# Moving the conversion of the first weights from the end of an attention phase to all of it

## The chip, the cores and the metric

One core of one Trainium2 chip runs the whole program. The metric is the device time of one execution in microseconds (us). The kernel before takes 809.04 us, the median of three runs (808.77 to 810.95).

## The reference, cut to what matters

Three layers follow each other, all in 32-bit floating point. The first is an attention in which a query sees only the keys that fall into the same cluster; then come two gated products of weights.

```python
# B, H, S, D = 2, 8, 768, 64; C = 16 clusters
q_assign = argmax((q / |q|) @ (centroids / |centroids|).T)      # the same for k
scores = where(q_assign == k_assign, q @ k.T / 8, -1e9)
attn = exp(scores - max(scores)) ; attn = attn / (sum(attn) + 1e-9)
x = attn @ v                                  # 1536 tokens x 512
h = (x @ w1) * (x @ w2) @ w3 @ w_out          # 512 -> 1024 -> 1024 -> 512
out = (sigmoid(h @ w_gate) * (h @ w_val)) @ w_out2
```

## The kernel before, in words

Every product is made from a high and a low part (`hi`, `lo`) of its operands, written as fp32r: three matmuls for a weight product (`mm3`), two for the others. `split` makes the two parts: a copy and a subtraction.

**The attention phase.** The 16 heads are taken in 8 pairs (`pr` 0 to 7). A pair has 6 blocks of 256 queries, so there are `NB` = 48 blocks (`i`), with two score tiles (`s`, 128 queries by 768 keys) each, 96 in all, 12 for a pair. For a score tile TensorE makes four matmuls (L328 to L331), VectorE takes the row maximum (`nm`, L332), ScalarE the exponential with its row sum (`e` and `ss`, L334). Two score tiles are then transposed on TensorE into three tiles `pt` (L345); ScalarE copies each to `ph` and VectorE subtracts to get `pl` (L56, L59), but one tile in two blocks of every pair goes by a copy `pc` to GpSimd. TensorE multiplies them by the values into `av` (L368, L369), ScalarE copies `av` to `xa` and `xb`. Beside this runs the preparation of the next pair: loading `raw` and `vraw`, splitting them (`prep_split`, `prep_v`), moving rows with DMAs of the SP queue into the operands QH, KH, QX, KX (`prep_scatter`), comparing with the centroids held in `cw` (`prep_sims`), and a one-hot code on VectorE that becomes part of QH and KH (`prep_argmax`, `prep_onehot`, `prep_mask`). At a pair's end `sums` turns the row sums `ss` into factors `r` by way of a transpose `rp`, a copy `rt`, a store and two loads; `finish_x` multiplies on GpSimd.

**The weights** come as 64-bit floats. `f64_steps` (L104) turns one array of 128 by 512 into a hi and a lo part. In the attention phase that is, for each of four arrays `w12_m_w`: an absolute value on ScalarE (L110), five VectorE instructions (L116, L119, L121, L123, L125), a sum on GpSimd (L127), a copy on ScalarE (L128), a subtraction on GpSimd (L129). Each `yield` lies behind a VectorE instruction, so one call of `convert` (L427) gives out one of these; 20 such instructions in all, and a 21st call that finishes the last array. The loop of L438 calls it twice a block from block 33 on. The first weight products need the four arrays, right behind the attention phase.

**What sets the order.** Each engine, and the SP queue, takes its instructions strictly in a fixed order. It isn't the order of the code: a scheduler sets it when the kernel is built, and `tc.issue_after(x)` keeps what stands under it behind `x`. PSUM holds two score tiles at a time (`ps_s`), three `pt` (`ps_t`) and one tile of `ps_a`, which `av` and `rp` share.

**The start.** VectorE makes `chi` and `clo` from the transposed centroids (L181, L182), GpSimd places them in `cw` with eight copies (L188), TensorE compares pair 0 with them (L265) between `warm` transposes that compute nothing.

**Afterwards.** From L488 on come the weight products, in which TensorE takes `p_0_0`, `p_1_0`, `p_0_1` and so on (`g_unit`, L529), two products of 12 matmuls each.

Of the kernel before, what the change touches and what calls it, by code (L numbers as in the profile page):

```python
# [12 lines left out]
ALU = mybir.AluOpType  # L13
# [14 lines left out]
def tile_cluster_attention__then__moe__then__gated_moe(  # L28
# [15 lines left out]
    nc = tc.nc  # L44
# [6 lines left out]
    def split(x, hi, lo, hi_engine, lo_engine):  # L51

        if hi_engine is nc.gpsimd:
            nc.gpsimd.tensor_scalar(out=hi, in0=x, scalar1=1.0, scalar2=1.0, op0=ALU.mult, op1=ALU.mult)  # L54
        elif hi_engine is nc.scalar:
            nc.scalar.copy(hi, x)  # L56
        else:
            nc.vector.tensor_copy(hi, x)
        lo_engine.tensor_tensor(out=lo, in0=x, in1=hi, op=ALU.subtract)  # L59
# [116 lines left out]
    cps = ps_a.tile([128, 128], F32, tag="a", name="cps")  # L176
    nc.tensor.transpose(cps, c2.rearrange("p j d -> p (j d)"), ident)
    warm(8, "warm1")
    chi = ctmp.tile([128, 128], F32R, name="chi")
    clo = ctmp.tile([128, 128], F32R, name="clo")  # L180
    nc.vector.tensor_copy(chi, cps)  # L181
    clo_done = nc.vector.tensor_tensor(out=clo, in0=cps, in1=chi, op=ALU.subtract)  # L182
    for e in range(2):
        rows = slice(64 * e, 64 * e + 64)
        for w in range(2):
            base = 64 * w + 32 * e
            for g, src in ((0, chi), (1, clo)):
                cw_done = nc.gpsimd.tensor_copy(  # L188
                    cw[rows, :, w, base + 16 * g : base + 16 * g + 16],
                    src[rows].bitcast(F32).rearrange("p (n e c) -> p n e c", n=NP, e=2)[:, :, e, :],  # L190
                )
# [8 lines left out]
    raw, last = {}, {}  # L200

    def load_qk(pr):
        for w in range(2):
            t = core.tile([128, S], F32, tag="raw", name=f"raw{pr}_{w}", bufs=2)
            last["SP"] = nc.sync.dma_start(t, qkT[pr, :, w, :])
            raw[pr, w] = t
# [16 lines left out]
    def prep_split(pr):  # L223
        qr, kr = raw.pop((pr, 0)), raw.pop((pr, 1))
        hl = []
        for w, t in ((0, qr), (1, kr)):
            hi = core.tile([128, S], F32R, tag="hi", name=f"hi{pr}_{w}", bufs=2)
            lo = core.tile([128, S], F32R, tag="lo", name=f"lo{pr}_{w}", bufs=2)
            if pr == 0 and w == 0:
                nc.scalar.activation(hi, t, AF.Copy, scale=0.125)  # L230
                nc.vector.scalar_tensor_tensor(out=lo, in0=t, scalar=0.125, in1=hi.bitcast(F32), op0=ALU.mult, op1=ALU.subtract)
                hl += [hi, lo]
                continue
            if w == 0:
                nc.gpsimd.tensor_scalar(out=t, in0=t, scalar1=0.125, scalar2=1.0, op0=ALU.mult, op1=ALU.mult)
            engines = (nc.scalar, nc.vector) if pr == 0 or w == 0 else (nc.gpsimd, nc.gpsimd)
            split(t, hi, lo, *engines)
            hl += [hi, lo]
        opnd[pr, "hl"] = hl
# [63 lines left out]
    def prep_v(pr):  # L303
        vr = raw.pop((pr, "v"))
        for e in range(2):
            vx = core.tile([128, KT, 2, D], F32R, tag="vx", name=f"vx{pr}_{e}", bufs=3)
            split(vr[:, e], vx[:, :, e, :], vx[:, :, 1 - e, :], nc.gpsimd, nc.gpsimd)
            opnd[pr, e, "v"] = vx
# [3 lines left out]
    NB = len(blocks)  # L312
# [72 lines left out]
    def sums(pr):  # L385

        ss = acc_x.pop((pr, "sum"))
        nc.vector.tensor_scalar(out=ss, in0=ss, scalar1=1e-9, scalar2=None, op0=ALU.add)
        nc.vector.reciprocal(ss, ss)
        rp = ps_a.tile([2 * KT, 128], F32, tag="a", name=f"rp{pr}")  # L390
        nc.tensor.transpose(rp, ss, ident)
        rt = core.tile([2 * KT, 128], F32, tag="rt", name=f"rt{pr}", bufs=1)
        nc.scalar.copy(rt, rp)  # L393
        nc.sync.dma_start(r_dram[pr], rt)
        r = core.tile([128, S], F32, tag="r", name=f"r{pr}", bufs=1)
        for e in range(2):
            row = r_dram[pr, KT * e : KT * e + KT, :].rearrange("t q -> (t q)")
            nc.sync.dma_start(r[64 * e : 64 * e + 64], row.unsqueeze(0).broadcast_to([64, S]))
        acc_x[pr, "r"] = r
# [5 lines left out]
        split(xa, x_hl[:, hp, 0, S * b : S * b + S], x_hl[:, hp, 1, S * b : S * b + S], nc.gpsimd, nc.gpsimd)  # L405


    with tc.issue_after(clo_done.ins):
        prep_split(0)
    prep_scatter(0, 0)  # L410
    prep_sims(0)
# [4 lines left out]
    prep_onehot(0)  # L416
    for e in range(2):
        prep_mask(0, e)
    with tc.issue_after(cw_done.ins):
        prep_v(0)  # L420
    load_qk(1)
    prep_split(1)
    prep_scatter(1, 0)
# [3 lines left out]
    def convert():  # L427

        while first or steps:
            if not steps:  # L430
                m, w = first.pop(0)
                hi, lo = (wt[m][:, p, w].rearrange("p k c -> p (k c)") for p in range(2))
                steps.append(f64_steps(raws.pop(0), hi, lo, f"w12_{m}_{w}", nc.gpsimd, nc.gpsimd))
            if next(steps[0], True) is None:
                return
            steps.pop(0)

    for i in range(-2, NB + 1):  # L438
        pr, at = divmod(i, 6)
        nxt = pr + 1 if 0 <= i and pr + 1 < NPR else None  # L440
        later = nxt + 1 if nxt and nxt + 1 < NPR else None
        scores(2 * i + 3)
        if nxt and at == 1:
            prep_scatter(nxt, 1)
            prep_argmax(nxt)
        transposes(i, 0)
        if nxt and at == 0:
            prep_sims(nxt)
        scores(2 * i + 4)
        if nxt and at == 2:  # L450
            prep_onehot(nxt)
            for e in range(2):
                prep_mask(nxt, e)
        transposes(i, 1)
        transposes(i, 2)
        if later and at == 2:
            load_qk(later)
        if later and at == 3:
            load_v(later)
        if i == 0:  # L460
            load_v(1)
        weighted_v(i - 1, 0)
        if nxt and at == 2:
            prep_v(nxt)
        weighted_v(i - 1, 1)
        if 0 < pr and i < NB and at == 2:
            finish_x(pr - 1)
        weighted_v(i - 1, 2)
        if later and at == 3:
            prep_split(later)  # L470
            prep_scatter(later, 0)
        if 0 <= i < NB and at == 5:
            sums(pr)

        if i == NB - 20:
            with tc.issue_after(last["SP"].ins):
                raws = [f64_load(w12[m, w], f"w12_{m}_{w}") for m, w in first[:3]]
        if i == NB - 10:
            raws.append(f64_load(w12[1, 1], "w12_1_1"))
        if NB - 15 <= i < NB:  # L480
            for _ in range(2):
                with tc.issue_after(last["DVE"].ins), tc.issue_after(last["ACT"].ins):
                    convert()
    finish_x(NPR - 1)
    att.close()

# [183 lines left out]
```

## Time and profile before

| | |
|---|---|
| median of 3 runs | 809.04 us |
| the profiled execution's own time | 808.15 us |
| its span on the core | 806.3 us |
| TensorE matmul, busy | 775.2 us (96%) |
| VectorE, busy | 578.7 us (72%) |
| ScalarE, busy | 360.4 us (45%) |
| GpSimd, busy | 342.7 us (43%) |

The shares are averages over phases with different limits. Matmuls are pipelined and their ends are modelled, so a busy TensorE is not one at its peak. The attention phase lasts to about 262 us. In the rows below PE is TensorE, PEld its weight loads, DVE VectorE, ACT ScalarE, POOL GpSimd, SPq the queue that issues DMAs; `<-` behind a wait names what ended it.

### The profile page before, as it was taken

Reading aid. Unit: us, or ns where it says so; the run is one execution under the profiler, and the core shown is the slowest. Engines: PE = TensorE matmul, PEld = TensorE weight load, DVE = VectorE, ACT = ScalarE, POOL = GpSimd, SP = SyncE. Lnnn points to the kernel's source line nnn. Section 1 sums busy time; section 2 is a strip of 40 time slices with the busy share of each in tenths; the row PEclk is TensorE's granted clock in tenths of the full one; section 3 lists DMA queues with packets and bytes.
Section 4 is the critical chain, followed back from the end, with each engine's and each line's share of the span. In section 5 each row is a group of like instructions: output and inputs, shape, how many; then the busy total and the mean of one; then the engine's idle time right before and its main releaser. Section 6 shows DMA issues by size and latency. Waiting matters only on the chain.

```text
span 806.3 us, 11235 instructions
## 1 busy us (share of the span) xinstructions
PE 775.2 (96%) x4051; PEld 660.6 (82%) x4051; DVE 578.7 (72%) x856; ACT 360.4 (45%) x711; POOL 342.7 (43%) x356
## 2 busy tenths in 40 slices
PE   7799999989889999999999999999999999999998
PEld 7688988988768888888888888888888888888886
DVE  5798999989998769998997532477751777827222
ACT  2688989888789433434443221332231222022100
POOL 4347667757675535454442200244421444124100
PEclk9999999999999999999999999999999999999999
DMA  8645656666621224343342100022230122200012
GB/s 217 152 125 131 164 139 169 150 171 178 165 72 47 73 80 156 132 152 135 131 138 99 52 1 1 27 78 80 79 104 1 59 99 79 79 1 0 1 66 91
DMA packets 26966, 78.04 MB, mean 97 GB/s; under 512 B 4416, under 2 KB 4512, under 8 KB 26912
## 3 DMA queue, kind: packets, MB, share of 16 engines
q1 hardware_dynamic: 26912, 77.33, 32.4%
q8 instruction: 32, 0.52, 0.3%
q14 instruction: 22, 0.18, 0.1%
HBM read 52.49 MB, written 3.19 MB: 69 GB/s over the span
## 4 chain that ended last, share of the span: by engine, by line
PE 69%; DVE 11%; POOL 6%; ACT 5%; DMA 4%; issue 3%; SPq 1%; DVEq 0%; POOLq 0%; ACTq 0%
PE p L67 18%; PE p L66 18%; PE p L65 18%; PE pt L345 3%; DVE nm L332 2%; PE s L328 2%; ACT e L334 2%; PE av L369 2%; DVE pl L59 1%; PE av L368 1%; PE s L330 1%; PE w34p L67 1%; ACT ph L56 1%; PE w34p L65 1%; PE sims L265 1%
## 5 line engine op out<-in xcount | busy, mean ns | idle before, releaser
L65 PE MATMUL p<-x,wgv 128*128 128x512 f32 x288 | 112.0, 389 | 0.0
L66 PE MATMUL p<-x,wgv 128*128 128x512 f32 x288 | 112.0, 389 | 0.0
L67 PE MATMUL p<-x,wgv 128*128 128x512 f32 x288 | 112.0, 389 | 0.0
L332 DVE TENSOR_REDUCE nm<-s 128x1 f32<-128x768 f32 x96 | 90.9, 948 | 12.0 <-PE s L331 11.6
L334 ACT ACTIVATE e<-s,nm 128x768 f32<-128x768 f32 x96 | 87.2, 909 | 6.5 <-DVE nm L332 5.6
L59 DVE TENSOR_TENSOR pl<-pt,ph 128x512 fp32r<-128x512 f32 x128 | 85.3, 681 | 5.3 <-ACT ph L56 4.5
L345 PE MATMUL pt<-ident,e 128*128 128x128 f32 x576 | 85.6, 281 | 2.8 <-DVE pl L59 2.6
L56 ACT CAST ph<-pt 128x512 fp32r<-128x512 f32 x128 | 73.0, 588 | 19.4 <-PE pt L345 13.5
L369 PE MATMUL av<-pl,vx 128*128 128x256 f32 x288 | 73.7, 288 | 5.5 <-POOL pl L59 5.2
L368 PE MATMUL av<-ph,vx 128*128 128x256 f32 x288 | 76.6, 298 | 0.5 <-ACT rt L393 0.5
L345 PEld LDWEIGHTS pt<-ident,e 128*128 128x128 f32 x576 | 69.7, 145 | 8.9 <-DVE pl L59 4.3
L66 PE MATMUL p<-x,w 128*128 128x512 f32 x192 | 74.8, 390 | 0.0
L67 PE MATMUL p<-x,w 128*128 128x512 f32 x192 | 74.7, 389 | 0.0
L65 PE MATMUL p<-x,w 128*128 128x512 f32 x192 | 74.7, 389 | 0.0
L54 POOL TENSOR_SCALAR u<-ut 128x512 fp32r<-128x512 f32 x36 | 22.3, 619 | 112.2 <-DVE ut L596 112.2
L66 PEld LDWEIGHTS p<-x,wgv 128*128 128x128 f32 x288 | 54.1, 188 | 11.3
L65 PEld LDWEIGHTS p<-x,wgv 128*128 128x128 f32 x288 | 54.1, 188 | 11.2
L67 PEld LDWEIGHTS p<-x,wgv 128*128 128x128 f32 x288 | 54.1, 188 | 11.2
L129 POOL TENSOR_TENSOR wo<-wo_a,wo 128x512 fp32r<-128x512 f32 x20 | 26.3, 1314 | 81.5 <-ACT wo L128 81.5
L369 PEld LDWEIGHTS av<-pl,vx 128*128 128x128 f32 x288 | 55.1, 191 | 7.0 <-POOL pl L59 6.9
L59 DVE TENSOR_TENSOR u<-ut,u 128x512 fp32r<-128x512 f32 x36 | 35.7, 991 | 34.1 <-POOL u L54 32.9
L596 DVE TENSOR_TENSOR ut<-p,ut 128x512 f32<-128x512 f32 x36 | 24.7, 686 | 44.4 <-PE p L67 44.3
(146 smaller groups left out, 1876.7 us busy)
## 6 DMA issues: line engine op xcount, KB each, us to landing
wgv_f<-in_w_gv_dram SPq DMA_DIRECT2D x24, 512.0 KB, 3.3
wo_f<-in_w_out_dram SPq DMA_DIRECT2D x20, 512.0 KB, 4.3
w_f<-in_w_dram SPq DMA_DIRECT2D x16, 512.0 KB, 3.2
w_f<-in_w3T_dram SPq DMA_DIRECT2D x16, 512.0 KB, 3.3
raw<-in_qkT_dram SPq DMA_DIRECT2D x16, 384.0 KB, 3.4
vraw<-in_v_dram SPq DMA_DIRECT2D x8, 384.0 KB, 4.6
QH<-hi SPq DMA_DIRECT2D x16, 192.0 KB, 2.5
KH<-hi SPq DMA_DIRECT2D x16, 192.0 KB, 2.5
```

Of the source, the lines that this page charges most:

```text
L56: nc.scalar.copy(hi, x)
L59: lo_engine.tensor_tensor(out=lo, in0=x, in1=hi, op=ALU.subtract)
L65: nc.tensor.matmul(ps, whi, xhi, start=start, stop=False)
L66: nc.tensor.matmul(ps, whi, xlo, start=False, stop=False)
L67: nc.tensor.matmul(ps, wlo, xhi, start=False, stop=stop)
L129: lo_engine.tensor_tensor(out=lo, in0=af, in1=hi, op=ALU.subtract)
L332: last["DVE"] = nc.vector.tensor_reduce(out=nm, in_=sp[:, 0:S], axis=AX.X, op=ALU.max, negate=True)
L334: last["ACT"] = nc.scalar.activation(et, sp[:, 0:S], AF.Exp, bias=nm, accum_out=ss[:, at : at + 1])
L345: nc.tensor.transpose(pt[:, kk, 128 * t : 128 * t + 128], es[t][:, k0 : k0 + 128], ident)
L368: nc.tensor.matmul(av, w, ph[:, kk, :], start=kt == 0, stop=False)
L369: nc.tensor.matmul(av, w, pl[:, kk, :], start=False, stop=kt == KT - 1)
L596: nc.vector.tensor_tensor(out=ut, in0=pv, in1=ut, op=ALU.mult)
```

## The change

The eight copies into `cw` go to VectorE. `sums` no longer adds and inverts `ss` ahead of the transpose: VectorE does both behind it, the addition reading `rp` in PSUM, and ScalarE's copy of `rp` goes. `convert` is called once in every second block from block 7 on, and the loads of its arrays are issued at blocks 4 and 24 in place of 28 and 38. What waited for `clo` now waits for the last copy into `cw`, and the first `prep_v` waits for none of them.

```diff
-    nc.vector.tensor_copy(chi, cps)
-    clo_done = nc.vector.tensor_tensor(out=clo, in0=cps, in1=chi, op=ALU.subtract)
+    split(cps, chi, clo, nc.vector, nc.vector)
...
-                cw_done = nc.gpsimd.tensor_copy(
+                cw_done = nc.vector.tensor_copy(
...
         ss = acc_x.pop((pr, "sum"))
-        nc.vector.tensor_scalar(out=ss, in0=ss, scalar1=1e-9, scalar2=None, op0=ALU.add)
-        nc.vector.reciprocal(ss, ss)
         rp = ps_a.tile([2 * KT, 128], F32, tag="a", name=f"rp{pr}")
         nc.tensor.transpose(rp, ss, ident)
         rt = core.tile([2 * KT, 128], F32, tag="rt", name=f"rt{pr}", bufs=1)
-        nc.scalar.copy(rt, rp)
+        nc.vector.tensor_scalar(out=rt, in0=rp, scalar1=1e-9, scalar2=None, op0=ALU.add)
+        nc.vector.reciprocal(rt, rt)
...
-    with tc.issue_after(clo_done.ins):
+    with tc.issue_after(cw_done.ins):
         prep_split(0)
...
-    with tc.issue_after(cw_done.ins):
-        prep_v(0)
+    prep_v(0)
...
-        if i == NB - 20:
+        if i == 4:
             with tc.issue_after(last["SP"].ins):
                 raws = [f64_load(w12[m, w], f"w12_{m}_{w}") for m, w in first[:3]]
-        if i == NB - 10:
+        if i == 24:
             raws.append(f64_load(w12[1, 1], "w12_1_1"))
-        if NB - 15 <= i < NB:
-            for _ in range(2):
-                with tc.issue_after(last["DVE"].ins), tc.issue_after(last["ACT"].ins):
-                    convert()
+        if 6 <= i < NB and i % 2:
+            with tc.issue_after(last["DVE"].ins), tc.issue_after(last["ACT"].ins):
+                convert()
```

The order moves with it. VectorE's queue in the sixth pair before, from the score tile 75 on; `nm` is a maximum, `pl` a subtraction of the attention, `w12` a conversion:

```order
L332 TENSOR_REDUCE nm75_3040<-s75_3041 128x1
L59 TENSOR_TENSOR pl36_0_3055<-pt36_0_3049,ph36_0_3054 128x512
L267 STREAM_TRANSPOSE sT7_3067<-sims7_3058 128x768
L59 TENSOR_TENSOR pl36_1_3086<-pt36_1_3080,ph36_1_3085 128x512
L332 TENSOR_REDUCE nm76_3071<-s76_3072 128x1
L59 TENSOR_TENSOR pl36_2_3095<-pt36_2_3089,ph36_2_3094 128x512
L119 TENSOR_SCALAR w12_0_1_a_3037<-w12_0_1_a_3037 128x512
L332 TENSOR_REDUCE nm77_3116<-s77_3117 128x1
L121 SCALAR_TENSOR_TENSOR w12_0_1_f64_2504<-w12_0_1_f64_2504,w12_0_1_a_3037 128x512
L276 TENSOR_REDUCE mx7_3135<-sm7_3069 128x24
L59 TENSOR_TENSOR pl37_0_3145<-pt37_0_3139,ph37_0_3144 128x512
```

Here a conversion stands behind nearly every maximum; pair 6 has 12 of the 20, pair 5 has 2 and pair 7 has 6. VectorE's queue of the change in the second pair, from the score tile 26 on, with the new `rt` (lines of the changed kernel lie up to four lower):

```order
L331 TENSOR_REDUCE nm26_1182<-s26_1183 128x1
L59 TENSOR_TENSOR lo3_0_1082<-raw3_0_991,hi3_0_1081 128x768
L121 SCALAR_TENSOR_TENSOR w12_0_0_f64_706<-w12_0_0_f64_706,w12_0_0_a_931 128x512
L331 TENSOR_REDUCE nm27_1234<-s27_1235 128x1
L390 TENSOR_SCALAR rt1_1226<-rp1_1224 12x128
L59 TENSOR_TENSOR pl12_0_1249<-pt12_0_1243,ph12_0_1248 128x512
L391 RECIPROCAL rt1_1226<-rt1_1226 12x128
L266 STREAM_TRANSPOSE sT3_1261<-sims3_1252 128x768
L331 TENSOR_REDUCE nm28_1265<-s28_1266 128x1
L59 TENSOR_TENSOR pl12_1_1280<-pt12_1_1274,ph12_1_1279 128x512
L59 TENSOR_TENSOR pl12_2_1289<-pt12_2_1283,ph12_2_1288 128x512
```

Conversions now stand four score tiles apart: 2 in pair 1 and 3 in each of the pairs 2 to 7. ScalarE's queue at the start before; `hi_0_295` is the high part of pair 1's queries, the `e` are the first exponentials:

```order
L297 CAST QH_1_260<-ohT_279 32x768
L56 CAST hi_0_295<-raw_0_291 128x768
L334 ACT_TABLE_LOAD
L334 ACTIVATE e_324,ss_316<-s_318,nm_317 128x768
L334 ACTIVATE e_333,ss_316<-s_327,nm_326 128x768
L334 ACTIVATE e_342,ss_316<-s_336,nm_335 128x768
```

And the same place of the change:

```order
L296 CAST QH_1_260<-ohT_279 32x768
L333 ACT_TABLE_LOAD
L333 ACTIVATE e_324,ss_316<-s_318,nm_317 128x768
L56 CAST hi_0_295<-raw_0_291 128x768
L333 ACTIVATE e_333,ss_316<-s_327,nm_326 128x768
L333 ACTIVATE e_342,ss_316<-s_336,nm_335 128x768
```

The table load and the first exponential stand ahead of the high part of pair 1.

## Rows read from the trace of the kernel before

**Rows 1.** The page, busy time, share of the span and instructions of each engine.
```profile
PE 775.2 (96%) x4051; PEld 660.6 (82%) x4051; DVE 578.7 (72%) x856; ACT 360.4 (45%) x711; POOL 342.7 (43%) x356
```

**Rows 2.** Stretches between the pairs' first maxima; columns in the first line.
```profile
core 0: us, PE busy (x) PEld busy (x) DVE busy (x) ACT busy (x) POOL busy (x), PEclk, DMA share, GB/s
51.63:234.39 182.76, 168.70 (x1208) 154.87 (x1209) 167.80 (x236) 156.27 (x343) 126.91 (x113) 0.98 0.61 156
137.87:166.27 28.40, 27.46 (x205) 25.41 (x204) 26.60 (x39) 25.46 (x57) 19.95 (x18) 1.00 0.61 153
197.96:234.39 36.43, 29.09 (x193) 25.70 (x191) 33.60 (x46) 27.58 (x59) 28.22 (x25) 0.95 0.54 141
234.39:262.00 27.61, 25.82 (x180) 22.33 (x178) 25.03 (x35) 24.79 (x56) 14.81 (x13) 1.00 0.15 53
300.00:320.00 20.00, 20.00 (x90) 16.56 (x89) 18.49 (x31) 8.34 (x14) 9.64 (x11) 1.00 0.39 132
```

**Rows 3.** Waits of VectorE, pairs 3 and 4: us in total, times, longest.
```profile
DVE lo L59 <- ACT hi L56: 1.7, 2, 0.8
DVE sT L267 <- PE sims L265: 0.6, 2, 0.4
```

**Rows 4.** Groups of VectorE's instructions, 0 to 262 us: busy us, mean ns, idle before.
```profile
L125 DVE SCALAR_TENSOR_TENSOR w_a<-w_f,w_a 128x512 f32<-128x512 uint32 x4 | 4.3, 1082 | 0.0
L119 DVE TENSOR_SCALAR w_a<-w_a 128x512 uint32<-128x512 uint32 x4 | 4.3, 1078 | 0.0
L388 DVE TENSOR_SCALAR ss<-ss 128x12 f32<-128x12 f32 x7 | 4.0, 570 | 0.0
L121 DVE SCALAR_TENSOR_TENSOR w_f<-w_f,w_a 128x512 uint32<-128x512 uint32 x4 | 3.1, 785 | 0.0
L123 DVE TENSOR_SCALAR w_a<-w_f 128x512 uint32<-128x512 uint32 x4 | 2.6, 655 | 0.0
L116 DVE TENSOR_SCALAR w_a<-w_a 128x512 f32<-128x512 f32 x4 | 2.1, 536 | 0.5 <-ACT w_a L110 0.5
L389 DVE RECIPROCAL ss<-ss 128x12 f32<-128x12 f32 x7 | 1.6, 225 | 0.2
L181 DVE CAST chi<-cps 128x128 fp32r<-128x128 f32 x1 | 0.3, 292 | 0.6 <-PE cps L177 0.6
L174 DVE RECIPROCAL nrm<-nrm 128x1 f32<-128x1 f32 x1 | 0.2, 165 | 0.0
```

**Rows 5.** VectorE in order of time, pair 6: start us, us, instruction.
```profile
212.42 2.07 DVE L119 TENSOR_SCALAR w_a<-w_a 128x512 uint32<-128x512 uint32 x1
...
219.46 1.17 DVE L123 TENSOR_SCALAR w_a<-w_f 128x512 uint32<-128x512 uint32 x1
...
230.54 1.10 DVE L121 SCALAR_TENSOR_TENSOR w_f<-w_f,w_a 128x512 uint32<-128x512 uint32 x1
```

**Rows 6.** Waits of TensorE in pair 6.
```profile
PE av L369 <- POOL pl L59: 2.8, 2, 1.7
```

**Rows 7.** In order of time, the start, all engines; in brackets the idle time before.
```profile
7.45 1.50 POOL L188 CAST cw<-clo 64x64 fp32r<-64x64 f32 x4
...
20.95 0.83 POOL L235 TENSOR_SCALAR raw<-raw 128x768 f32<-128x768 f32 x1 [8.98 <-DMA vraw<-in_v_dram]
...
21.81 0.83 ACT L56 CAST hi<-raw 128x768 fp32r<-128x768 f32 x1 [1.74 <-POOL raw L235]
...
22.67 1.47 DVE L59 TENSOR_TENSOR lo<-raw,hi 128x768 fp32r<-128x768 f32 x1 [0.57 <-ACT hi L56]
...
23.95 0.90 ACT L334 ACTIVATE e<-s,nm 128x768 f32<-128x768 f32 x1
...
26.14 0.96 DVE L332 TENSOR_REDUCE nm<-s 128x1 f32<-128x768 f32 x1 [2.00 <-PE s L331]
```

**Rows 8.** In order of time, the end of the attention phase.
```profile
269.44 0.39 PE L65 MATMUL p<-x,w 128*128 128x512 f32 x1
...
276.14 1.86 POOL L59 TENSOR_TENSOR x<-xa,x 128x768 fp32r<-128x768 f32 x1
```

## The prediction

> **What bounds the kernel now.** I read the busy times of the page first: TensorE is busy for 96% of the span, VectorE for 72% [rows 1]. These are means over two different programs, so the next view is busy time by stretches, cut at each pair's first maximum [rows 2]. Behind the attention phase, from 300 to 320 us for instance, TensorE is busy for all 20.00 us: the weight products are bound by TensorE, and the change leaves them alone. What can move is when they begin, thus the length of the attention phase.
>
> In that phase a quiet pair (pair 4) lasts 28.40 us, with VectorE busy for 26.60, TensorE for 27.46 and ScalarE for 25.46: three engines close to full, none with room for much. Pair 6 holds 12 of the 20 conversion instructions and lasts 36.43 us, 8.0 more; VectorE is busy for 33.60 of them, 7.0 more. So a conversion isn't free beside the attention. Pairs 1 to 6 take 182.76 us together, 12.4 more than six pairs of 28.40. Third I read who waits in the quiet pairs: VectorE waits 1.7 us over two pairs for the high part of the next queries and 0.6 us for the comparison with the centroids, 1.15 us a pair [rows 3]. Both are waits for other engines that VectorE finds less of when it comes later; a dense packing of conversions in one pair can use them only once, a spread one in every pair.
>
> **The change part by part.** *Conversions.* By groups, the 20 VectorE instructions cost 4.3, 4.3, 3.1, 2.6 and 2.1 us in fours, 16.4 in all or 0.82 each [rows 4]. Their number stays. Their places: before 0 in pairs 1 to 4, 2 in pair 5, 12 in pair 6, 6 in pair 7; now 2 in pair 1 and 3 in each later one, so 17 in pairs 1 to 6 and 3 in pair 7. Six quiet pairs are 6 x 28.40 = 170.4 us; 17 x 0.82 = 13.9 come on top, and 6 x 1.15 = 6.9 go into the waits. I take the whole of 1.15, since the two waits are for engines that the conversions don't delay; bounds are 0 and 1.15 used.
>
> *The sums.* Before, an addition of 0.57 us and a reciprocal of 0.225 on 128 x 12 [rows 4]. Now both work on 12 rows of 128. The addition reads PSUM, for which the nearest row is the cast of `cps`, 0.29 us [rows 4]. No row has a reciprocal of 128 columns: with 1 column it takes 0.165 us, with 12 0.225 [rows 4], so 0.225 is the lower bound and the straight line, 0.165 + 127 x 0.0055 = 0.86, the upper. I take 0.86, because the width is what grew. That is 0.29 + 0.86 - 0.57 - 0.225 = +0.36 us a pair on VectorE, 6 x 0.36 = 2.1 (lower bound: 6 x -0.28 = -1.7). ScalarE loses a copy, which I count as nothing, since VectorE is the fuller of the two. New is that the one `ps_a` tile is freed by VectorE: `av` of the next block waits behind `rt`, which waits behind one maximum; I cost that at nothing, since TensorE has transposes queued ahead of it, and at 0.95 us a pair (a maximum, as in the last row of [rows 7]) if it hasn't.
>
> The Trainium skill ("VectorE: DVE Perf Modes", section "First, the fixed hardware budget") says that a reciprocal is an iterative division with a repeat count of 8. At the 0.96 GHz that the page gives, 128 columns would be an estimated 1.07 us and the sum 6 x 0.21 = 1.3 us higher; no run shows such a reciprocal yet.
>
> Pairs 1 to 6 then take 170.4 + 13.9 - 6.9 + 2.1 = 179.5 us in place of 182.76: -3.3.
>
> *Pair 7* loses 3 of 6 conversions, 2.5 us of VectorE. Its stretch is 27.61 us with TensorE busy for 25.82 [rows 2], so between 0 and 1.8 can go; I take the middle, -0.9. Its last conversion now stands close to the end and the array is finished behind the last exponential. That is needed by the second pair of products only: each takes 24 matmuls, and TensorE begins them at 269.44 [rows 8]. The last `x` must be there for the third; GpSimd ends it at 278.0 [rows 8], and two times 24 matmuls at 20.00 / 90 = 0.222 us [rows 2] end at 280.1. `r` of pair 7 may come 0.9 us later, by the longer sums; 1.2 us would be left. Nothing for the end, then.
>
> *The start.* ScalarE runs the high part of pair 1 (21.81, 0.83 us), then a table load, then the first exponential at 23.95 [rows 7]; that high part waits for GpSimd's scaling at 20.95, which waited 8.98 us for a DMA. In the new order the table load and the first exponential run while that DMA is on its way. The third maximum, at 26.14, waited 2.00 us for the scores, which wait for the first exponential to free PSUM. Now it is held by the subtraction `lo` ahead of it, which ends at 22.67 + 1.47 = 24.14 [rows 7]. So -2.0 us for all that follows. Bounds: 0, if pair 0 is held up later by pair 1's preparation, and -3.5, if that DMA lands sooner too.
>
> *The copies of the centroids.* GpSimd ends them at 8.95 [rows 7]. On VectorE eight of them at no more than the 0.29 us of `chi` [rows 4] are 2.3 us. The subtractions of pair 0 now stand behind them, so up to 2.3 us could be lost, or 0.7 won; I take 0, because the DMA that the start waits for until 20.95 covers both.
>
> *The loads.* 1.5 MB now stand ahead of pair 0's store of `rt` in SP's queue, and GpSimd waits for `r` in pair 1. In the new order of GpSimd the tile `pl` that TensorE needs stands ahead of that wait; 0, and +1.7 us (its longest wait on such a tile, [rows 6]) if a later one is caught.
>
> The sum: -3.3 - 0.9 - 2.0 = -6.2 us against the profiled execution's 808.15 us (span 806.3 and 1.85 around it), 801.95. The median lies 0.89 us above that execution, so 802.8 us.
>
> **The rivals.** *Each conversion costs its full time wherever it stands.* For it: VectorE grew by 7.0 us in pair 6 and the pair by 8.0. Against it: the waits of [rows 3]. Then the 6.9 us aren't won: 809.7 us, no change; only the start and pair 7 pay for the new conversions.
>
> *The conversions vanish.* If the spread ones stand where VectorE would have waited anyway, for TensorE's scores for instance, pairs 1 to 6 take 170.4 + 2.1 = 172.5, and the time is 808.15 - 10.3 - 2.9 + 0.89 = 795.8 us. Against it: VectorE's idle time in a quiet pair is 1.8 us, less than three times 0.82.
>
> *GpSimd holds VectorE's conversions up, in every pair* (slower). Three conversions of pair 6 took 2.07, 1.17 and 1.10 us [rows 5], where GpSimd was busy for 28.22 of 36.43 us [rows 2]. At their mean of 1.45 us, and with no wait used, 17 of them make 24.6 us: 170.4 + 24.6 + 2.1 = 197.1, which gives 820.4 us. The kernel is slower by 0.3% from 188.1 us on, that is when a conversion costs more than 0.92 us and nothing goes into waits, or more than 1.32 if all of it does. Against it: the mean of 0.82 holds such cases already, and GpSimd is freer in the quiet pairs (19.95 of 28.40). Beside this, the Trainium skill ("SBUF — State Buffer", section "Who interferes with whom") says that VectorE's copies and tensor-scalar operations on SBUF, in a two-port mode, and those with two SBUF inputs share a locked port pair with GpSimd and block for the whole of its instruction; by that rule such a stall may strike in any pair, and the 2.07 us agree with it.
>
> **How the numbers follow.** Chances: the forecast 0.56, full cost 0.20, vanishing 0.13, held up 0.11. About 0.3%, 2.4 us, is what a measurement of this kernel can tell from none. The forecast's own range, from half the waits unused and no gain in pair 7 to a start of -3.5, is 798 to 807; nearly all of it is faster. Full cost lies about no change, with a fifth on either side. So faster 0.68, same 0.17, slower 0.15. The range 797.5 to 809.7 leaves out most of the held-up case and the vanishing one.
>
> **What would show it.** In the profile of the changed kernel: the first exponential ahead of the high part, before 21.8 us, and the third maximum near 24.1; pairs 1 to 6 near 29.9 us each, pair 6 as short as pair 2, without TensorE's waits for GpSimd's `pl` there; VectorE's waits for `hi` and the comparison near 0; reciprocals of 0.86 us; the weight products starting near 263 us. The prediction is wrong if quiet pairs grow by more than 2.5 us, if conversions of 2 us are common, or if pair 0 stays at 31 us.

## The result and the profile after

The changed kernel takes 814.58 us, the median of 6 runs (812.91 to 817.8); the kernel before took 809.67 beside it (6 runs, 808.77 to 811.16). The ratio is 1.0062 with a 95% interval of 1.0036 to 1.0087: it is slower by 0.6%. The forecast was 802.8 us, faster, with a range up to 809.7; it was wrong in sign and the time lies outside the range. The profiled execution took 815.58 us, its span 813.7.

The page, busy times of the changed kernel [rows 1]:

```profile
PE 782.9 (96%) x4051; PEld 661.0 (81%) x4051; DVE 588.1 (72%) x864; ACT 360.0 (44%) x703; POOL 341.4 (42%) x348
```

VectorE is busy for 9.4 us more, and TensorE, with the same 4051 matmuls, for 7.7 us more. The next view shows stretches of the changed kernel, each from one pair's first maximum to another's, in the columns of [rows 2]: pairs 1 to 6, pair 4, pair 6, and pair 7 to its last maximum.

```profile
51.28:242.31 191.03, 175.28 (x1208) 154.48 (x1208) 177.59 (x241) 157.04 (x338) 129.80 (x116) 0.99 0.59 152
146.33:178.77 32.44, 29.35 (x202) 25.86 (x203) 29.73 (x42) 26.28 (x58) 22.36 (x20) 1.00 0.56 140
210.06:242.31 32.25, 29.03 (x202) 25.54 (x202) 29.44 (x42) 26.91 (x59) 23.20 (x22) 1.00 0.54 128
242.31:265.96 23.65, 23.18 (x169) 21.03 (x168) 22.21 (x31) 22.10 (x51) 9.53 (x8) 1.00 0.07 18
```

Pair 6 is shorter, as forecast (32.25 us, 36.43 before), but no pair is as short as the quiet ones were: pair 4 went from 28.40 to 32.44, and pairs 1 to 6 from 182.76 to 191.03. The attention phase loses its time there, 8.3 us. VectorE's busy time in pairs 1 to 6 grew by 9.8 us, and its idle time there hardly fell, from 14.96 to 13.44. Its waits in pairs 3 to 5 (total us, times, longest; [rows 3]) say the same:

```profile
DVE lo L59 <- ACT hi L56: 2.4, 3, 0.9
DVE pl L59 <- ACT ph L56: 2.4, 4, 0.7
DVE nm L331 <- PE s L330: 1.2, 3, 0.8
```

The wait for `hi` is 0.8 us a pair, what it was. The groups of VectorE's instructions from 0 to 275 us, to be read against [rows 4], with the mean ns behind the comma:

```profile
L391 DVE RECIPROCAL rt<-rt 12x128 f32<-12x128 f32 x8 | 7.5, 932 | 0.0
L121 DVE SCALAR_TENSOR_TENSOR w_f<-w_f,w_a 128x512 uint32<-128x512 uint32 x4 | 5.7, 1435 | 0.0
L123 DVE TENSOR_SCALAR w_a<-w_f 128x512 uint32<-128x512 uint32 x4 | 4.7, 1168 | 0.0
L125 DVE SCALAR_TENSOR_TENSOR w_a<-w_f,w_a 128x512 f32<-128x512 uint32 x4 | 4.5, 1132 | 0.0
L116 DVE TENSOR_SCALAR w_a<-w_a 128x512 f32<-128x512 f32 x4 | 3.5, 882 | 1.2 <-ACT w_a L110 1.2
L119 DVE TENSOR_SCALAR w_a<-w_a 128x512 uint32<-128x512 uint32 x4 | 3.4, 850 | 0.0
L390 DVE TENSOR_SCALAR rt<-rp 12x128 f32<-12x128 f32 x8 | 2.2, 276 | 1.8 <-PE rp L388 1.8
```

The 20 conversion instructions take 21.8 us, 1.09 each, against 16.4 and 0.82 before. Eight of them took longer than 1.1 us, and seven of these began behind a GpSimd instruction with two inputs that was still running; I call that the hold-up. Two lines of pair 3 in order of time show one:

```profile
132.29 1.83 POOL L402 TENSOR_TENSOR xa<-xa,r 128x768 f32<-128x768 f32 x1 [0.22 <-DMA r<-r_dram]
...
132.98 1.43 DVE L119 TENSOR_SCALAR w_a<-w_a 128x512 uint32<-128x512 uint32 x1
```

So the sum for pairs 1 to 6 seems to close: 170.4 us of quiet pairs, 17 conversions of 1.11 us (18.8 us in this stretch) and six sums longer by 0.41 make 191.7, and 191.03 was measured. That would be the rival in which GpSimd holds VectorE up, at a lower price. The experiments show that it isn't the cause.

### The profile page after: what moved, and what is told of

It reads as the page before. It is cut to its first block, busy times and chain, and to the rows that moved or that the text cites. A ratio compares the mean times of both kernels' runs of the same rounds, so it can differ in the third digit from the quotient of the medians.

```text
span 813.7 us, 11221 instructions
## 1 busy us (share of the span) xinstructions
PE 782.9 (96%) x4051; PEld 661.0 (81%) x4051; DVE 588.1 (72%) x864; ACT 360.0 (44%) x703; POOL 341.4 (42%) x348
## 4 chain that ended last, share of the span: by engine, by line
PE 65%; DVE 13%; POOL 7%; ACT 5%; issue 4%; DMA 4%; SPq 0%; DVEq 0%; POOLq 0%; ACTq 0%
PE p L66 17%; PE p L67 17%; PE p L65 17%; DVE nm L331 2%; PE pt L344 2%; DVE pl L59 2%; ACT e L333 2%; PE s L327 2%; PE w34p L67 1%; DMA raw<-in_qkT_dram 1%; PE w34p L65 1%; PE w34p L66 1%; ACT ph L56 1%; DMA wo_f<-in_w_out_dram 1%; PE av L368 1%
## 5 line engine op out<-in xcount | busy, mean ns | idle before, releaser
L344 PE MATMUL pt<-ident,e 128*128 128x128 f32 x576 | 89.2, 279 | 6.8 <-ACT pc L350 3.1
L368 PE MATMUL av<-pl,vx 128*128 128x256 f32 x288 | 75.4, 291 | 0.6 <-POOL pl L59 0.4
L67 PEld LDWEIGHTS p<-x,wgv 128*128 128x128 f32 x288 | 54.1, 188 | 11.2
L66 PEld LDWEIGHTS p<-x,wgv 128*128 128x128 f32 x288 | 54.1, 188 | 11.2
L367 PEld LDWEIGHTS av<-ph,vx 128*128 128x128 f32 x288 | 54.8, 190 | 1.8 <-DVE rt L390 0.8
```

Source lines behind the costliest of these rows:

```text
L66: nc.tensor.matmul(ps, whi, xlo, start=False, stop=False)
L67: nc.tensor.matmul(ps, wlo, xhi, start=False, stop=stop)
L344: nc.tensor.transpose(pt[:, kk, 128 * t : 128 * t + 128], es[t][:, k0 : k0 + 128], ident)
L367: nc.tensor.matmul(av, w, ph[:, kk, :], start=kt == 0, stop=False)
L368: nc.tensor.matmul(av, w, pl[:, kk, :], start=False, stop=kt == KT - 1)
```

## The experiments

Times are medians of each call's runs; a difference is between the medians, against the kernel before on the same chip in the same call. The ratio, with its 95% interval behind it, comes from all runs of both kernels and not from the medians, so the two can differ slightly.

**Which part of the change.** The three parts alone, and the change without one of them. The diffs are against the kernel before and cut to a line each.

```diff
 start_only (with what waits for the copies):
-                cw_done = nc.gpsimd.tensor_copy(
+                cw_done = nc.vector.tensor_copy(
 sums_only; after_old_sums is the changed kernel with this undone:
-            nc.scalar.copy(rt, rp)
+            nc.vector.tensor_scalar(out=rt, in0=rp, scalar1=1e-9, scalar2=None, op0=ALU.add)
 spread_only (with the loads at blocks 4 and 24):
-        if NB - 15 <= i < NB:
+        if 6 <= i < NB and i % 2:
```

Expected of start_only: 

> The kernel before with the start of the change alone (copies of the centroids on VectorE, what waits for them, the order of the first exponentials that follows). My theory now: the gain at the start is nearly all lost before pair 1, because the raw DMA lands later; 0.4 us faster than before (809.67), 809.3 us. Rival, the forecast's own step: 2.0 us faster, 807.7 us.

Expected of sums_only: 

> The kernel before with the new sums alone. My theory: VectorE has no time left, so the addition and the wide reciprocal (0.28 and 0.93 us in the changed kernel, 0.57 and 0.23 before) cost 0.41 us in each of six or seven pairs, 2.5 to 2.9 us: 812.3 us. Rival: they lie beside other work and the copy that ScalarE loses pays for them, 809.7 us.

Expected of spread_only: 

> The kernel before with the spread conversions alone (loads at blocks 4 and 24, one call in every second block from 7). My theory: the spread ones meet GpSimd's instructions at fixed places of every pair and take 1.1 us each in place of 0.8, about 5 us more VectorE time, of which pair 7 gives some back: 2.8 us slower, 812.5 us. Rival: place does not matter, 810 us, and the loss of the whole change is in the sums. Second rival: all of the loss is here, 814.6 us.

Expected of after_old_sums: 

> The changed kernel with the old sums. My theory: 2.5 us faster than the changed kernel (814.58), 812.1 us. Rival, that the sums cost nothing: 814.5 us. Second rival, that they are the whole loss: 809.7 us or less.

Measured: start_only 807.68, -0.7 us (0.9986, 0.9973 to 0.9999); sums_only 811.65, +3.2 (1.0045, 1.003 to 1.006); spread_only 815.21, +6.8 (1.0083, 1.0064 to 1.0102); after_old_sums 815.15, +6.7 (1.0077, 1.0055 to 1.0098). The start is worth a third of what I forecast, the sums cost about what their instructions say, and the spreading loses the most. But the parts don't add up: -0.7 + 3.2 + 6.8 is 9.3, the whole change costs 4.9, and taking the sums out of it wins nothing. Costs that are paid by the instruction would add up. And in spread_only the 20 conversions are not long at all, 13.7 us or 0.68 each. Its pairs 1 to 6, in the columns of [rows 2]:

```profile
51.85:242.96 191.11, 174.43 (x1200) 154.28 (x1201) 170.80 (x240) 157.51 (x343) 127.87 (x115) 0.98 0.59 152
```

They are 8.35 us longer than before, with VectorE busy for 3.0 us more; its time can't be the whole cause. The loss lies in pairs 3 and 4, of 34.9 and 34.6 us. In order of time, pair 3 of spread_only, idle time before in brackets:

```profile
117.81 0.83 POOL L54 TENSOR_SCALAR hi<-raw 128x768 fp32r<-128x768 f32 x1 [2.70 <-issue]
118.72 1.81 POOL L59 TENSOR_TENSOR lo<-raw,hi 128x768 fp32r<-128x768 f32 x1
...
120.59 0.49 PE L265 MATMUL sims<-lo,cw 128*128 128x512 f32 x1 [1.05 <-POOL lo L59]
...
121.71 0.98 DVE L267 STREAM_TRANSPOSE sT<-sims 128x768 f32<-128x768 f32 x1 [2.64 <-PE sims L265]
```

TensorE comes to the comparison of the next pair before GpSimd has the operands ready (1.05 us of waiting), and VectorE waits for TensorE (2.64 us).

**Is it VectorE's time?** The five VectorE instructions of a conversion are left out, of the changed kernel and of the one before, or replaced by reductions; and the conversions are moved by one block.

```diff
 after_none, before_none, in f64_steps, for each of the five:
-            nc.vector.tensor_scalar(out=af, in0=af, ...)
             yield
 after_reduce:
+                nc.vector.tensor_reduce(out=mm[:, k : k + 1], in_=af, axis=AX.X, op=ALU.max)
                 yield
 even:
-        if 6 <= i < NB and i % 2:
+        if 6 <= i < NB and i % 2 == 0:
```

Expected of after_none: 

> The changed kernel without the five VectorE instructions of each conversion of a weight (the weights' high and low words are then used unconverted; the GpSimd addition and subtraction, ScalarE's copies and the loads stay). If VectorE's time is what the change lost (pairs 1 to 6 of the changed kernel, 191.0 us, are six quiet pairs of 28.40, 17 conversions of 1.09 and six longer sums), those pairs fall to about 173 us, pair 7 by up to 2, and the time to 795 us, at or below the old order without those instructions. If the loads and the conversions' GpSimd and ScalarE parts, which now stand in pairs 1 to 5, delay the next pair's preparation, two or three pairs stay at 31 us or more, and the time at 803 us or above, 6 us or more over the old order without them.

Expected of before_none: 

> The kernel before without the same five VectorE instructions of each conversion. The 12.4 us by which pairs 1 to 6 exceed six quiet pairs should go, and up to 1.8 us of pair 7: 795 to 797 us, by either theory. It is what the changed kernel without them is compared with.

Expected of after_reduce: 

> The changed kernel with each of the 20 conversion instructions replaced by a VectorE maximum over the same 128 x 512 (one input, 128 x 1 out; the weights are not converted): a like number of instructions of about 0.6 us that need no second input. If the 1.09 us of a conversion is waiting for GpSimd's two-input instructions, pairs 1 to 6 lose 17 x 0.45 = 7.7 us and the time is about 807 us. If the conversions cost by being in the way of the next pair's preparation, however long they are, it stays within 2 us of the changed kernel: 812 to 816 us.

Expected of even: 

> The changed kernel with a conversion in every even block in place of every odd one, so that none stands in the block in which GpSimd multiplies xa by r right behind it. If hold-up by that multiplication is what made the conversions long, most of them take 0.41 to 0.68 us and the time falls by 4 to 7 us, to 807 to 810. If the place does not matter, only the number of conversions a pair, it stays at 813 to 816 us.

Measured: after_none 811.63 (+2.8; 1.0043, 1.002 to 1.0066), before_none 804.17 (-4.7; 0.9947, 0.993 to 0.9963), after_reduce 816.79 (+8.0; 1.01, 1.0075 to 1.0126), even 815.85 (+7.0; 1.0092, 1.0064 to 1.012). Without any of the 20 instructions the change still costs 7.5 us over the kernel before without them. The scheduler placed each of these kernels anew, so the order isn't held in them. Pairs 1 to 6 of after_none, in the columns of [rows 2]:

```profile
50.36:238.42 188.06, 173.69 (x1204) 155.03 (x1205) 161.91 (x223) 157.07 (x339) 129.84 (x117) 0.98 0.60 157
```

The same of after_reduce, and its 17 reductions in that stretch:

```profile
51.81:241.57 189.76, 176.06 (x1208) 155.71 (x1208) 168.56 (x239) 156.79 (x340) 127.75 (x117) 0.98 0.59 153
```

```profile
L118 DVE TENSOR_REDUCE w_m<-w_a 128x1 f32<-128x512 f32 x17 | 11.3, 666 | 0.4 <-ACT w_a L110 0.4
```

VectorE is busy for 15.7 and 9.0 us less than in the changed kernel, and the pairs are shorter by only 3.0 and 1.3: the rest turned into idle time (26.2 and 21.2 us, from 13.4). So neither VectorE's fullness nor the hold-up sets the time, and my theory that each conversion costs its whole 1.09 us fell, with its 795 and 807 us. Moving the conversions by one block won nothing either (even). My rival, that loads and the conversions' GpSimd and ScalarE parts delay the preparation of the next pair, fits after_none, but it doesn't say why the three parts of the change don't add up.

**The order of the instructions.** The next place to look is the order in the built programs, which the traces show too. TensorE's steps in pair 3, S a score tile, T0 to T2 the three tiles of transposes, V0 to V2 the products with the values, C the comparison with the centroids, R the transpose of the sums:

```
before        S V1 V2 S T0 T1 T2 S T2 V0 V1 V2 S T0 C R C T1 S T2 V0 V1 V2 S T0 S T1 T2 V0 V1 V2 S T0 S T1 T2 V0 V1 V2 S T0 S T1 T2 V0 V1 V2 S T0 T1 T2 V0
changed       S T0 S T0 T1 V0 T2 V1 S V1 V2 S T0 R T0 T1 T2 C T2 V0 S V0 V1 V2 S T0 V0 T1 S T1 T2 V0 V1 V2 T0 S T0 V0 V1 T1 V1 S T2 V1 V2 T0 S T0 T1 S T2 V0 V1 V2 S T0 V0 V1 T1 V1 T2 V1 V2
```

Before, pairs 2 to 4 go in the round S T0 S T1 T2 V0 V1 V2, and so do all later pairs if the conversions and their loads are left out of the program. With conversions in pairs 6 and 7 those leave it. In the changed kernel, spread_only, even, after_none and after_reduce hardly one such round is left in pairs 2 to 6. In sums_only the pairs go in another round, and its pairs 2 to 4 take 28.95, 28.97 and 30.07 us, so another round on TensorE need not cost much. An instruction added on one engine, or a sum moved to another, thus shifts the rows of engines on which nothing was edited. New theory: the time is lost by the order, not by the added work.

First I tied TensorE's steps to the order of the code, which is that round throughout.

```diff
-        transposes(i, 0)
+        pin(transposes, i, 0)        # issued behind TensorE's last instruction; so for scores and weighted_v
```

Expected of pin_after: 

> The changed kernel, with TensorE's score, transpose and value steps of the attention loop tied to the order of the code (each step behind the one before it), which is the order that the kernel before has in pairs 2 to 4 and the changed kernel has in no pair. If the loss is the order that the scheduler makes once the conversions and the longer sums are in, it goes: pairs 1 to 6 at 28.40 each, 17 conversions of 0.82 and six longer sums of 0.41 are at most 186.8 us, 4.2 less than in the changed kernel, and the time 810 us or less; with part of the conversions beside waits 803. If the conversions and sums themselves cost what was lost, whatever TensorE's order, it stays at 813 to 816 us.

Expected of pin_before: 

> The kernel before with the same tie. Its pairs 2 to 4 have that order but at the pairs' ends; pairs 6 and 7 have not. By the theory of the order pair 6 (36.43 us) and pair 7 shorten and the rest stays: 802 to 808 us. By the rival, no change: 807 to 811 us. It is also what the tied kernels are compared with.

Expected of pin_after_none: 

> The changed kernel with the same tie and without the five VectorE instructions of each conversion (weights unconverted). Untied and without them it took 811.6 us, against 804.2 for the kernel before without them. By the theory of the order the tie removes that difference: six pairs of 28.4 to 29 us, 795 to 800 us. By the rival (loads and the conversions' GpSimd and ScalarE parts cost the time in the quiet pairs) it stays above 808 us.

Expected of pin_spread: 

> The changed kernel with the old sums (addition and reciprocal of 128 x 12 ahead of the transpose) and the same tie: the new start and the spread conversions only. By the theory of the order it is the best of these: pin_after less 6 x 0.41 = 2.5 us, 801 to 808 us. Untied it took 815.2 us; by the rival it stays at 812 us or more.

Measured: pin_after 819.33 (+11.2; 1.014, 1.0105 to 1.0176), pin_before 812.06 (+3.9; 1.0056, 1.0035 to 1.0077), pin_after_none 814.66 (+6.5; 1.0086, 1.0059 to 1.0113), pin_spread 812.43 (+4.3; 1.0057, 1.0031 to 1.0084). None of the times that I expected by the new theory came. Tying TensorE's steps is slower in itself, and the other engines' rows were still the scheduler's. What is left is a difference: with the tie on both sides the start and the spreading cost 0.4 us (812.43 against 812.06), in place of 6.7 (after_old_sums); the sums, though, cost 6.9.

Then I wrote down the whole order: for every engine and the SP queue, the places that the scheduler gives the attention phase's instructions when the conversions and their loads are left out (with the new start). Each instruction is tied behind its predecessor in that list; conversions, their loads and, in kept_after, the sums' VectorE instructions are left to the scheduler.

```diff
+    for engine, runs in KEPT.items():
+        mine = [x for x in traced if str(x.engine) == "EngineType." + engine and type(x).__name__.startswith("Inst") and x.name not in free]
+        row = [mine[k] for first_k, n in runs for k in range(first_k, first_k + n)]
+        for a, b in zip(row, row[1:]):
+            tc.add_manual_dep(b, a.name, mybir.DependencyInfo(mybir.DependencyClass.NoSync, mybir.DependencyReason.DATA), reason="kept order")
```

Expected of kept_packed: 

> The new start and the old, packed conversions; every engine and the SP queue take all other instructions of the attention phase in one written-down order, that which the scheduler makes when there are no conversions at all (its pairs 2 to 6 are all in the order of the quiet pairs of the kernel before). Scheduled freely it took 807.7 us. If the scheduler's order after conversions begin costs time, pairs 6 and 7 shorten: pair 6 to 28.4 + 12 x 0.82 = 38 at the most if all conversions cost their time, 33 if half of them lie in waits; time 800 to 808. If the order does not matter: 807 to 809.

Expected of kept_spread: 

> The new start and the spread conversions, old sums, in the same written-down order, with the conversions at the same scores as in the changed kernel. Scheduled freely the spread conversions took 815.2 us. If the order is what cost the time, pairs 1 to 6 come to at most 170.4 + 17 x 0.82 = 184.3 us and with waits used to 177.4: 798 to 806 us, below the kernel before. If the conversions themselves cost it (2.3 us in each pair, whatever the order), it stays at 811 us or above.

Expected of kept_after: 

> The whole change (start, sums, spread conversions) in the written-down order; only the sums' VectorE instructions and the conversions are placed by the scheduler. By the theory of the order it is kept_spread plus 6 to 7 times the 0.41 us of the longer sums: 800 to 809 us, at least 6 us below the changed kernel. By the rival it stays at 812 us or above. Tied on TensorE alone the sums cost 6.9 us; if that comes from the one av tile that waits behind them, kept_after lies 5 us or more above kept_spread.

Expected of kept_none: 

> kept_spread without the five VectorE instructions of each conversion (weights unconverted). Its distance to kept_spread is what these 20 instructions cost in a fixed order: 16.4 us of VectorE time; 14 us or more if each costs its full time, 7 if half lies in waits, under 3 if they lie in waits altogether. By the theory of the order it takes 794 to 799 us; if it stays above 805 the loads and the GpSimd and ScalarE parts cost time in themselves.

Measured: kept_packed 811.59 (+3.0; 1.0041, 1.0025 to 1.0057), kept_spread 805.25 (-3.4; 0.9967, 0.9951 to 0.9983), kept_after 807.27 (-1.3; 0.9999, 0.998 to 1.0017), kept_none 802.06 (-6.6; 0.9928, 0.9903 to 0.9953). The whole change goes from 1.0062 to 0.9999, clear of the noise of both, with the same work on every engine and the conversions at the same scores; the spreading goes from 1.0083 to 0.9967, of which the new start explains 0.0014. kept_spread beats both kernels. Pairs 1 to 6 of kept_after:

```profile
47.83:232.13 184.30, 168.34 (x1191) 151.51 (x1192) 170.79 (x240) 156.80 (x337) 131.75 (x115) 0.99 0.61 157
```

And of kept_spread, to be read against 191.11 us in spread_only:

```profile
47.66:231.05 183.39, 167.41 (x1191) 151.54 (x1192) 168.79 (x240) 156.99 (x343) 131.05 (x115) 0.99 0.61 158
```

kept_after's pairs are 6.7 us shorter than the changed kernel's, and VectorE is busy for 6.8 us less in them with the same instructions. Its conversions there [rows 4]:

```profile
L125 DVE TENSOR_SCALAR w_a<-w_a 128x512 f32<-128x512 f32 x4 | 3.4, 856 | 0.8 <-ACT w_a L119 0.6
L128 DVE TENSOR_SCALAR w_a<-w_a 128x512 uint32<-128x512 uint32 x4 | 3.4, 846 | 0.0
...
L132 DVE TENSOR_SCALAR w_a<-w_f 128x512 uint32<-128x512 uint32 x3 | 2.8, 941 | 0.0
L130 DVE SCALAR_TENSOR_TENSOR w_f<-w_f,w_a 128x512 uint32<-128x512 uint32 x3 | 2.4, 796 | 0.0
L134 DVE SCALAR_TENSOR_TENSOR w_a<-w_f,w_a 128x512 f32<-128x512 uint32 x3 | 2.2, 723 | 0.0
```

They are 14.2 us, 4.6 less; the comparison in `prep_argmax` (`sm`) is 1.7 us less and that in `prep_onehot` (`oh`) 0.5. So the order decides how often GpSimd holds VectorE up. In spread_only 5.7 of the 7.7 us that kept_spread wins in pairs 1 to 6 are VectorE's idle time instead (20.3 us, 14.6 in kept_spread), while kept_spread's 17 conversions are longer (16.2 us, 11.5 in spread_only). One cause, the order, shows in two forms. kept_packed says that the written order is not good in itself: with packed conversions it costs 3.7 us over start_only (+3.0 against -0.7). In it, spreading them is worth 6.3 us (811.59 to 805.25).

The granted clock doesn't explain the gain of kept_after: over all runs it is 0.994 on average in kept_after and in the changed kernel, and it was 0.99 in pairs 1 to 6 of both traces. Ahead of pair 1 the two traces do differ, with 0.90 in the changed kernel and 1.00 in kept_after, whose pair 1 begins 3.5 us earlier; how much of that is the clock's, no run shows. kept_packed's runs had 0.989 on average, against 0.992 in start_only and 0.994 in kept_spread, and in one kernel the runs at a lower clock are longer (kept_after: 805.57 us at 0.997, 810.21 at 0.991). So its 3.7 and 6.3 us are in part the clock's.

kept_none tells what the 20 VectorE instructions cost when all others keep their order. It took 802.06 us, 3.2 less than kept_spread, and missed the 794 to 799 that I expected by the theory of the order. Its pairs 1 to 6:

```profile
49.73:229.12 179.39, 165.54 (x1191) 151.47 (x1192) 157.59 (x223) 156.80 (x343) 129.67 (x116) 0.99 0.63 165
```

Against it kept_spread has 11.2 us more of VectorE's time in these pairs, and they are 4.0 us longer: about 7 us of the conversions lie where VectorE would have waited. But with no conversion instruction on VectorE at all, six pairs still take 9.0 us more than six times 28.40. Pairs 1 (32.06 us) and 6 (31.28) hold 6.5 of that; whether the loads, the conversions' GpSimd and ScalarE parts or something else lengthens them, no run shows.

Last, which engine's order it is: the list on TensorE alone, and on all but TensorE.

```diff
 kept_pe:   KEPT = {"PE": ...}
 kept_rest: KEPT = {"DVE": ..., "Activation": ..., "Pool": ..., "SP": ...}
```

Expected of kept_pe: 

> The whole change with the written-down order on TensorE alone; the other engines and the SP queue take theirs from the scheduler, which sees TensorE's. If TensorE's order is what costs the time (in the changed kernel its transposes wait 6.8 us for emptied tiles and are busy for 67.3 us in pairs 1 to 6, against 0.0 and 60.0 in kept_after), it comes to 806 to 809 us, as kept_after. If it is the order of the others (VectorE, GpSimd, SP), it stays at 812 us or above, as the kernel tied on TensorE in the code's order did.

Expected of kept_rest: 

> The whole change with the written-down order on all engines but TensorE. If TensorE's order is what costs the time: 811 us or more, with transposes that still wait. If it is the others' (above all which VectorE instruction meets which of GpSimd): 806 to 809 us. Between the two, both matter.

Measured: kept_pe 813.01 (+4.2; 1.0051, 1.0033 to 1.0069), kept_rest 810.76 (+2.0; 1.0033, 1.0015 to 1.0051). TensorE's transposes in pairs 1 to 6 of the changed kernel (busy us, mean ns, idle before):

```profile
L344 PE MATMUL pt<-ident,e 128*128 128x128 f32 x434 | 67.3, 276 | 6.8 <-ACT pc L350 3.1 <-DVE pl L59 2.7 <-ACT e L333 1.0
```

And of kept_pe:

```profile
L351 PE MATMUL pt<-ident,e 128*128 128x128 f32 x429 | 59.7, 273 | 0.8 <-ACT pc L357 0.5 <-DVE pl L64 0.3
```

Transposes pulled ahead of the values' products wait for tiles that ScalarE and VectorE have not emptied, and the written order on TensorE takes that away. But the time stays: kept_pe's waits move to the scores (12.4 us for the exponential, 5.6 in the changed kernel). My reading that TensorE's transposes were the price fell. Neither list alone gives back the whole: by the ratios TensorE's gives 0.0011, the others' 0.0029, both 0.0063. The first is within the noise and the second at its edge, so how the gain divides between the engines isn't shown. Which single inversion in the rows counts most stays open.

## Why the prediction was wrong, point by point

**The step that failed** is the base of the sum: "Six quiet pairs are 6 x 28.40 = 170.4 us", with conversions and sums as terms on top. It took the length of one quiet pair for all six, and for any order of the instructions. Without a single conversion instruction on VectorE, pairs 1 to 6 take 188.06 us in the scheduler's order of the change (after_none), 17.7 more than 170.4. In the written-down order they take 179.39 (kept_none). Of the 8.7 us between the two, six longer sums are 2.5 by their instructions; the other 6.2 are, as an estimate, the order's, and the whole change wins 6.7 us there by the written order (191.03 to 184.30). The remaining 9.0 us are a second fault of the base, which gave all six pairs the length of a short one: pair 1 took 29.82 us before, without any conversion, and 32.06 in kept_none. The edits made the scheduler leave the order of the quiet pairs. The listing of both programs was there to be compared; I compared it at the edited places only.

- *Conversions, 17 x 0.82.* Their duration was 1.11 us in pairs 1 to 6 of the changed kernel, 0.84 in kept_after (14.2 / 17) and 0.95 in kept_spread. The Trainium skill ("SBUF — State Buffer", section "Who interferes with whom") lets VectorE's two-input operations, and its copies and tensor-scalar operations in a two-port mode, block behind GpSimd; the 1.43 us beside L402 agrees. But a duration is no price: after_reduce has 9.0 us less of VectorE time in pairs 1 to 6 than the changed kernel and is not faster. That a conversion costs time beside the attention I had read from pair 6, longer by 8.0 us with 7.0 more of VectorE's time. Without the VectorE instructions (before_none, where the order isn't held either) that pair is only 1.8 us shorter:

```profile
197.71:232.32 34.61, 29.61 (x197) 25.32 (x195) 26.94 (x39) 28.10 (x60) 27.07 (x25) 0.97 0.56 150
```

- *6.9 us into waits.* Of the 11.2 us that the conversions add to VectorE in the kept order about 7 went into waits, so there this term came out: 13.9 - 6.9 was to be 7.0 us of length, and 4.0 were measured, with 11.2 in place of 13.9. In the changed kernel the sum with no wait used closes, at 191.7, only because its base was too small: leaving out 15.7 us of VectorE's time won 3.0.
- *The sums, +0.36 a pair.* Measured 0.276 + 0.932 - 0.570 - 0.225 = +0.41. With the order kept they cost 2.0 us by the medians (807.27 against 805.25) and 2.6 by the ratios, as 6 x 0.41 = 2.5 should; scheduled freely 3.2. TensorE's wait of `av` for `rt`, which I put at nothing, came once in pairs 1 to 6, for 0.6 us. The reciprocal of 128 columns took 0.93 us; I had said 0.86 by the straight line. The Trainium skill ("VectorE: DVE Perf Modes", section "First, the fixed hardware budget") gave an estimated 1.07 by its repeat count; the measurement lies between.
- *Pair 7, -0.9.* From first to last maximum 26.21 us before, 23.65 now: -2.6, more than the most I allowed for. The end keeps some of that gain: the phase starts pair 7 7.9 us later, the unbroken row of weight products begins at 275.24, 5.8 us later than in [rows 8] (three of its matmuls stand a little ahead in both kernels), and the span is 7.4 us longer. The 1.6 us lost behind that arise between 372 and 378 us, where the first product of `w3` and `w_out` (`w34p`) waits for its weights; from 365 to 385 us:

```profile
PE w34p L67 <- POOL w L129: 1.1, 2, 0.6
```

  In the kernel before it waits there 0.2 us, once.
- *The start, -2.0.* The first exponential came ahead of the high part, and the third maximum earlier, at 24.83. In order of time [rows 7]:

```profile
18.94 0.47 PE L329 MATMUL s<-KX,QX 128*128 128x512 f32 x1 [1.51 <-DMA QX<-lo]
...
20.56 0.90 ACT L333 ACTIVATE e<-s,nm 128x768 f32<-128x768 f32 x1 [1.65 <-DVE nm L331]
...
22.22 0.83 POOL L234 TENSOR_SCALAR raw<-raw 128x768 f32<-128x768 f32 x1 [3.71 <-DMA raw<-in_qkT_dram]
...
23.95 0.96 DVE L59 TENSOR_TENSOR lo<-raw,hi 128x768 fp32r<-128x768 f32 x1 [2.34 <-ACT hi L56]
...
24.83 0.95 DVE L331 TENSOR_REDUCE nm<-s 128x1 f32<-128x768 f32 x1
```

  GpSimd's scaling, held by its load, began 1.3 us later than before, so the maximum gained 1.3 and not 2.0, and pair 1 begins at 51.28 in place of 51.63: only 0.35 is left. That is near the lower bound, "if pair 0 is held up later by pair 1's preparation"; start_only gives -0.7 us. The granted clock in pair 0 was 0.84, against 0.95 before, so a part may have been lost by it; no run separates the two. The copies into `cw` take 8 x 0.19 us and cost nothing that shows.
- *The rivals.* The one that GpSimd holds VectorE up had the sign, and with 1.1 us in place of 1.45 it would have had the size in pairs 1 to 6; it named a symptom. That the conversions nearly vanish came closest in the kept order, 3.2 us for all 20. That the order itself moves was among none of them.
- *The signs of being wrong.* Two of the three came: pair 4 grew by 4.0 us, and pair 0 took 31.7 us. Conversions of 2 us were not common, two of 20.

## What to carry to other kernels

Where a scheduler places the instructions, an edit can change the whole order. Before adding prices to a stretch's length, compare the full rows of every engine in stretches that the edit doesn't touch; if the round has changed, the old length is no base. Leaving instructions of the busiest engine out is a cheap test of whether their time is the cost at all, and a clean one only with the order of all others held (kept_none against kept_spread). An order can be written down: here the same change went from 0.6% slower to no difference, and its start and spreading, in the kept order, to 0.3% faster than the kernel before. That order was not better for every kernel: with packed conversions it was 0.4% slower than the kernel before.

## What the runs showed of the hardware that was not expected

Leaving 15.7 us of VectorE's work out of pairs 1 to 6, in which VectorE was 93% busy, shortened them by 3.0 us (after_none), and with the order held 11.2 us were worth 4.0 (kept_none against kept_spread). A busy share of 93% thus said little of what the work costs. And the same transposes, 72 a pair, kept TensorE busy for 67.3 us in the changed kernel and for 59.7 to 60.3 in kept_pe, kept_after and kept_spread, at a mean of 273 to 276 ns each. As the ends of matmuls are modelled, such a difference of busy time need not be work: kept_pe has the lower one and is not faster.
